# One more staging buffer, one more weight buffer and a new order for a chunked-attention and MoE kernel

## The chip, the cores and the metric

One Trainium2 chip, one of its cores. The metric is the device time of one execution in microseconds (us). Of the kernel before, three timed runs took 683.93, 684.89 and 685.61 us; the median is 684.89 us.

## The reference

Three stages follow each other, all in float32. The weights of the two feed-forward stages come to the kernel as 64-bit floats.

```
# 4 batches, 8 heads, 768 steps, 40 per head: gated recurrent attention
m_new = max(f + m, i); C = exp(f + m - m_new) * C + exp(i - m_new) * v k^T; n likewise with k
y = sigmoid(o_gate) * (C q) / max(|n q|, 1)
x = y as 3072 tokens x 320
x = ((x @ w1) * (x @ w2)) @ w3 @ w_out                          # d_ff 1024
out = max(max(x @ u1, x @ u2), x @ u3) @ u_out                  # d_ff 768
```

## The kernel before

**Units and visits.** The recurrence is done in chunks of 87 steps (`L`), nine per batch (the ninth has 72), so 36 units. `visit(v)` is one TensorE step: the scores of unit v (line 738) and the outputs and carried state of unit v - 1 (line 747). Both write one PSUM tile, `aq` (for the first odd units `acs`). DVE then multiplies the scores of unit v by its decays (line 772, into `pk`), which frees the tile for the scores of the next visit, and forms `y` from the outputs of unit v - 1 (lines 795 to 798; the gate is line 805, the copy of 64 columns lines 810 and 811). `pk` also needs the carried part, lines 696 and 705, on POOL or DVE. TensorE turns `y` (line 818), and ACT and DVE split the turned columns into a high and a low part (lines 836 and 839): these are the tokens of the feed-forward stages, in blocks of 384.

**Decays.** The gates of all 32 sequences are scanned on DVE at the start (lines 491 to 525). The result goes to DRAM (`d_na`, line 529), one batch of it comes back (line 561) and is split (lines 562 and 563), and the first nine units get their decays by matmuls (lines 656 and 657, the constant `one` from line 535) and an exponential on ACT (line 660). The other units load `d_na` (line 665) and use lines 670, 676 and 679.

**Weights.** A `granule` is 512 KB of 64-bit weights: one load (line 1050) into a staging buffer, two ACT steps or one ACT and one DVE step (lines 1055, 1061 or 1064), and a join on DVE (line 1072). Staging buffers are `sx` (three, only until the first switch of pools) and `stg` (three). `w3 @ w_out` is multiplied out on the chip: `fold(ft)`, eight times, each in two pieces of four float32 matmuls (line 1122); a piece needs one joined granule of `w3` in one of four buffers (`L_BUFS`), the first two pieces also the five granules of `w_out` in `wof`. Lines 1129 and 1133 empty each fold. The other weights are split into high and low parts (lines 1082 and 1085, 1097 and 1104).

**Feed-forward.** For each block of 384 tokens, groups of eight matmuls (lines 857 to 862) give the products with w1 and w2, or with u1 to u3; lines 903 and 905, or 931 and 934, combine them, lines 884 and 888 split the result, and lines 967 to 971 (first stage) or 986 (second) multiply on. `LATE`: weights of the second stage take the place of the pools `early` and `first` once nothing uses those (`late_w`).

**What sets the order.** Nothing is issued where the code stands. Every step is recorded by `Plan.op` with its engine, cost and dependencies, and `Plan.run` then walks a model of the engines and of the transfers (SP issues all of them from one queue; `LAND` is its time from the bus to the landing) and takes, on each free engine, the ready step of the lowest rank. `PRIO` holds a rank for each of 1963 steps, `PICK` a digit for each step that two engines can do. Each engine, SP too, executes its list in that order. The model's TensorE clock (`clock`) is slow up to a fixed time and full after it.

Of the kernel before, what the change touches and what calls it, by code (L numbers as in the profile page):

```python
# [43 lines left out]
EX = 3  # L44
L_BUFS = 4
# [11 lines left out]
LAND = 900  # L57
# [5 lines left out]
    "11011100110101111000011010001110000011001001110010100111001101101101011000000010111110111101001010111000110001"  # L63
    "00111001101101011010110001101100111100000110000111111101001111110011010111111100010100011110001100110011101101"
    "01011101001000101001110110101010100101111001110010000100011110001100101111001000010000010100000110100101111000"
    "10000000000111100000011100111110001001111010110101011000"
)
PRIO = (
# [100 lines left out]
def act(n, psum=False):  # L169
    return (51 if psum else 93) + 0.8333 * n  # L170
# [184 lines left out]
def mlstm_moe_kernel(  # L355
# [103 lines left out]
    for k_, n in (("msk", NCH * L), ("ff", NCH * L), ("aug", NCH * 128), ("git", NCH * L), ("gft", NCH * L)):  # L459
# [3 lines left out]
        for tag, (x, y) in where.items():  # L463
            if x < o + n and o < y:
                over[tag].append(("g", k_))
        o += n
    made["rv", 0], made["cr", 0] = misc[:, 0:8 * L], misc[0:L, o:o + 128 + LE]
    for tag, (x, y) in where.items():
        if x < 8 * L:
            over[tag].append(("rv", 0))  # L470
# [872 lines left out]
```

## Time and profile before

| | |
|---|---|
| three runs, median | 684.89 us (683.93 to 685.61) |
| profiled execution, its own time | 686.26 us |
| span of the profiled execution | 684.3 us |
| TensorE matmul (PE) busy | 655.6 us, 96% |
| weight load (PEld) busy | 621.1 us, 91% |
| DVE, ACT, POOL busy | 360.0, 296.8, 198.3 us |
| bytes moved | 76.09 MB, mean 111 GB/s |

Times inside the profile count from its first instruction; the profiled execution took 1.96 us more than its span, and 1.37 us more than the median. PE is the engine that matters, so the table is to be read by stretches of time and not by engine: where PE sits idle, and where its clock (PEclk, in tenths of 2.4 GHz) is below full. In the second table of the profile, the span in 40 slices of 17.1 us, PE is below nine tenths in the first, second, fifth and sixth slice and in the last, and PEclk in the fifth; the transfers keep their engines busy by seven tenths or more in the first five slices and by less after that.

### The profile page before, as it was taken

How to read it: one execution, taken by the hardware profiler on the slowest of the kernel's cores; microseconds unless marked ns; L12 is line 12 of the kernel's file. 1: busy time of each engine (PE TensorE's matmuls, PEld its weight loads, DVE VectorE, ACT ScalarE, POOL GpSimd, SP SyncE). 2: the span in 40 equal slices, each digit the busy share in tenths (PEclk: the TensorE clock that was granted, in tenths of full speed). 3: DMA queues.
4: the chain of work that ended last, by engine and by line, in shares of the span. 5: the costliest groups of instructions: out<-in, count | busy, mean ns of one | idle time of the engine just before them, and what ended most of it. 6: DMA issues, size and time to landing. Idle time of an engine off the chain costs nothing.

```text
span 684.3 us, 14869 instructions
## 1 busy us (share of the span) xinstructions
PE 655.6 (96%) x6217; PEld 621.1 (91%) x6217; DVE 360.0 (53%) x717; ACT 296.8 (43%) x572; POOL 198.3 (29%) x195
## 2 busy tenths in 40 slices
PE   3899889999999999999999999999999999999997
PEld 2577789999999999999999999999999999999997
DVE  7578797698745584453444464543345461312332
ACT  6856767677631345341423335344333232323202
POOL 1015444555421145122232353233232421010000
PEclk9999899999999999999999999999999999999999
DMA  8999735456322154221123172232032200000001
GB/s 304 330 330 368 252 115 182 148 185 187 110 83 95 55 159 148 84 83 41 44 83 113 46 210 88 64 104 76 8 112 84 86 8 1 2 1 0 1 1 58
DMA packets 25887, 76.09 MB, mean 111 GB/s; under 512 B 3260, under 2 KB 6899, under 8 KB 25820
## 3 DMA queue, kind: packets, MB, share of 16 engines
q1 hardware_dynamic: 25820, 75.14, 33.9%
q8 instruction: 48, 0.79, 0.5%
q14 instruction: 19, 0.16, 0.1%
HBM read 71.10 MB, written 4.03 MB: 110 GB/s over the span
## 4 chain that ended last, share of the span: by engine, by line
PE 83%; DMA 5%; DVE 5%; ACT 3%; issue 2%; POOL 1%; SPq 0%; ACTq 0%; POOLq 0%; DVEq 0%
PE wk L857 13%; PE wk L858 12%; PE wk L859 12%; PE acs L986 9%; PE wk L860 6%; PE wk L862 5%; PE acs L967 4%; PE acs L971 4%; PE wk L1122 4%; PE aq L747 3%; PE acs L969 3%; PE aq L738 3%; PE wk L872 1%; PE wk L818 1%; DMA sx<-in_wo 1%
## 5 line engine op out<-in xcount | busy, mean ns | idle before, releaser
L884 ACT CAST ph<-misc 128x384 fp32r<-128x384 f32 (+1 forms) x114 | 57.6, 508 | 169.2 <-PE acs L986 72.3
L888 POOL TENSOR_TENSOR pl<-misc,ph 128x384 fp32r<-128x384 f32 (+1 forms) x60 | 63.4, 1057 | 229.8 <-ACT ph L884 224.8
L934 DVE TENSOR_TENSOR misc<-misc,wk 128x384 f32<-128x384 f32 (+1 forms) x98 | 53.2, 545 | 104.5 <-PE wk L862 77.7
L857 PE MATMUL wk<-xh,wch 128*128 128x384 f32 x288 | 98.4, 342 | 1.7 <-DVE misc L934 1.0
L858 PE MATMUL wk<-xh,wcl 128*128 128x384 f32 x288 | 96.9, 336 | 0.0
L859 PE MATMUL wk<-xl,wch 128*128 128x384 f32 x288 | 96.8, 336 | 0.0
L857 PE MATMUL wk<-xh,wah 128*128 128x384 f32 x256 | 89.2, 349 | 2.6 <-DVE misc L905 1.1
L858 PE MATMUL wk<-xh,wal 128*128 128x384 f32 x256 | 87.0, 340 | 0.0
L859 PE MATMUL wk<-xl,wah 128*128 128x384 f32 x256 | 86.9, 339 | 0.0
L905 DVE TENSOR_TENSOR misc<-misc,wk 128x384 f32<-128x384 f32 x64 | 35.2, 551 | 81.6 <-PE wk L862 39.8
L857 PEld LDWEIGHTS wk<-xh,wch 128*128 128x128 f32 x288 | 54.1, 188 | 4.0 <-DVE misc L934 2.0
L903 ACT COPY misc<-wk 128x384 f32<-128x384 f32 x64 | 30.4, 476 | 61.5 <-PE wk L862 40.1
L888 DVE TENSOR_TENSOR pl<-misc,ph 128x384 fp32r<-128x384 f32 (+1 forms) x54 | 32.5, 604 | 44.6 <-ACT ph L884 44.4
L858 PEld LDWEIGHTS wk<-xh,wcl 128*128 128x128 f32 x288 | 54.1, 188 | 0.0
L859 PEld LDWEIGHTS wk<-xl,wch 128*128 128x128 f32 x288 | 54.1, 188 | 0.0
L857 PEld LDWEIGHTS wk<-xh,wah 128*128 128x128 f32 x256 | 48.8, 191 | 4.7 <-DVE misc L905 1.8
L1122 PE MATMUL wk<-wof,w 128*128 128x320 f32 x128 | 40.4, 472 | 12.6 <-DVE w L1072 11.7
L986 PE MATMUL acs<-wd,ph 128*128 128x320 f32 x288 | 51.0, 311 | 0.6 <-ACT misc L1028 0.5
L858 PEld LDWEIGHTS wk<-xh,wal 128*128 128x128 f32 x256 | 48.8, 191 | 0.0
L859 PEld LDWEIGHTS wk<-xl,wah 128*128 128x128 f32 x256 | 48.8, 191 | 0.0
L860 PE MATMUL wk<-xh,wcr 128*128 128x384 f32 x144 | 48.4, 336 | 0.0
L1122 PEld LDWEIGHTS wk<-wof,w 128*128 128x128 f32 x128 | 25.8, 206 | 23.5 <-DVE w L1072 11.8
(147 smaller groups left out, 1317.8 us busy)
## 6 DMA issues: line engine op xcount, KB each, us to landing
kv<-in_kv SPq DMA_DIRECT2D x32, 672.0 KB, 5.2
raw<-in_qk SPq DMA_DIRECT2D x36, 348.0 KB, 4.6
dd<-d_na SPq DMA_DIRECT2D x24, 348.0 KB, 4.0
sx<-in_w3t SPq DMA_DIRECT2D x9, 512.0 KB, 6.6
stg<-in_wc SPq DMA_DIRECT2D x9, 512.0 KB, 4.2
out<-misc SPq DMA_DIRECT2D x24, 160.0 KB, 2.2
stg<-in_w3t SPq DMA_DIRECT2D x7, 512.0 KB, 8.5
stg<-in_wa SPq DMA_DIRECT2D x5, 512.0 KB, 6.1
```

Of the source, the lines that this page charges most:

```text
L857: PE.matmul(p, lhsT=h_[:, kt], rhs=xh[:, kt], start=kt == 0, stop=False)
L858: PE.matmul(p, lhsT=l_[:, kt], rhs=xh[:, kt], start=False, stop=False)
L859: PE.matmul(p, lhsT=h_[:, kt], rhs=xl[:, kt], start=False, stop=False)
L860: PE.matmul(p, lhsT=r_, rhs=xh[:, 2], start=False, stop=False)
L862: PE.matmul(p, lhsT=r_, rhs=xl[:, 2], start=False, stop=True)
L884: P.op("A", act(n), lambda sl=sl: A.copy(out=T("ph", key)[:, sl], in_=T(*src)[:, sl]), r=[src + part], w=[("ph", key) + part])
L888: e.tensor_tensor(out=T("pl", key)[:, sl], in0=T(*src)[:, sl], in1=T("ph", key)[:, sl].bitcast(F32), op=ALU.subtract)
L903: P.op("A", act(TB, True), lambda: A.copy(out=T(*sa), in_=T(*ps[0])), r=[ps[0]], w=[sa])
L905: P.op("V", dve(TB), lambda: V.tensor_tensor(out=T(*sa), in0=T(*sa), in1=T(*ps[1]), op=ALU.mult), r=[ps[1]], w=[sa])
L934: P.op("V", dve(sl.stop - sl.start), lambda sl=sl: V.tensor_tensor(out=T(*sc)[:, sl], in0=T(*sc)[:, sl], in1=T(*ps)[:, sl], op=ALU.max), r ...
L986: PE.matmul(T(f"ac{m}", (k, 1)), lhsT=src[:, m * 128:m * 128 + 128], rhs=w[:, o:o + DM], start=first_, stop=last_,)
L1122: PE.matmul(T(*ps), lhsT=T(*w3)[:, i * 128:i * 128 + 128], rhs=wof[:, gt * 320:gt * 320 + 320], start=gt == 0, stop=gt == 7,)
```

## The change

`EX` goes from 3 to 4 and `L_BUFS` from 4 to 5: a fourth `sx` staging buffer and a fifth buffer for joined `w3`. The fourth `sx` lies in the pool `first`, so that the gate of the second set of late weights now also waits for the last use of `sx`. The load of the constants `sel` and its tile get 96 rows in place of 87. `LAND` goes from 900 to 1300, the modelled cost of the `kv` load from 1.3 to 1.36 per element, and `PICK` and `PRIO` are replaced in full. The columns recorded with a visit (`cols`) are not read by `run`.

```diff
-EX = 3
-L_BUFS = 4
+EX = 4
+L_BUFS = 5
...
-LAND = 900
+LAND = 1300
...
-    "11011100110101111000011010001110000011001001110010100111001101101101011000000010111110111101001010111000110001"
+    "10110100100101010111000001100000100101110111110011010011011011100000111101110010111101010110110010011011100100"
...
-    27, 139, 164, 433, 293, 56, 36, 192, 232, 29, 10, 114, 554, 467, 59, 73, 329, 383, 395, 148, 303, 652, 287, 664,
...
-        (early, "sx", EX, 1024), (tmp, "w3", L_BUFS, 512), (tmp, "raw0", RAW0, 8 * L),
+        (early, "sx", 3, 1024), (tmp, "sx", EX - 3, 1024), (tmp, "w3", L_BUFS, 512), (tmp, "raw0", RAW0, 8 * L),
...
-        slots[tag] = [pool_.tile([128, n], F32, name=f"{tag}{i}") for i in range(bufs)]
+        slots.setdefault(tag, []).extend(pool_.tile([128, n], F32, name=f"{tag}{pool_.id}_{i}") for i in range(bufs))
...
-    made["rv", 0], made["cr", 0] = misc[:, 0:8 * L], misc[0:L, o:o + 128 + LE]
+    made["rv", 0], made["cr", 0] = misc[:, 0:8 * L], misc[0:LP, o:o + 128 + LE]
...
-        dma(1.3 * m, lambda: SP.dma_start(out=T("kv", q)[:, 0:m], in_=kv[b, c, :, 0:m]), w=[("kv", q, x) for x in "kgx"])
+        dma(1.36 * m, lambda: SP.dma_start(out=T("kv", q)[:, 0:m], in_=kv[b, c, :, 0:m]), w=[("kv", q, x) for x in "kgx"])
...
-                if key[0] in (("raw", "sg", "w3", "wo", "mp") if q else ("hl", "one", "sx")):
+                if key[0] in (("raw", "sg", "sx", "w3", "wo", "mp") if q else ("hl", "one", "sx")):
...
-    sel = np.eye(L, 128 + LE, dtype=f)
-    sel[:, 128:] = np.where(np.arange(L)[:, None] > np.arange(LE), f(-1e30), f(0))
+    sel = np.eye(LP, 128 + LE, dtype=f)
+    sel[:, 128:] = np.where(np.arange(LP)[:, None] > np.arange(LE), f(-1e30), f(0))
```

The lists keep their lengths (PE 3171 rows, DVE 687, SP 183), and nearly every row moves. Of the steps that two engines can do, DVE now has 19 of line 696 (14 before), 56 of line 888 (52), 14 of line 705 (13), 17 of line 805 (20) and 7 of line 1029 (14). Three places follow; in the new kernel a tile's name also carries the number of its pool (`sx78_0` is the first `sx`, `w366_0` the first buffer of joined `w3`, `wk61_1` the second `wk`).

DVE at the start, from the join of the first `w_out` granule (`wof`) on; `w30` is the first joined `w3`, `mp` and lines 515 to 521 are the end of the gate scan. Before:

```order
L1072 SCALAR_TENSOR_TENSOR wof_75<-sx0_107 128x512
L506 SCALAR_TENSOR_TENSOR misc_122<-misc_122 32x783
L1072 SCALAR_TENSOR_TENSOR wof_75<-sx1_108 128x512
L1064 TENSOR_SCALAR sx2_109<-sx2_109 128x512
L1072 SCALAR_TENSOR_TENSOR w30_110<-stg2_106 128x512
L1072 SCALAR_TENSOR_TENSOR wof_75<-sx2_109 128x512
L515 SCALAR_TENSOR_TENSOR mp_76<-misc_122,mp_76 32x9
L525 COPY misc_122<-mp_76 32x9x41
L521 TENSOR_TENSOR misc_122<-misc_122,mp_76 32x783
```

and now:

```order
L1072 SCALAR_TENSOR_TENSOR wof_75<-sx78_0_107 128x512
L506 SCALAR_TENSOR_TENSOR misc_124<-misc_124 32x783
L515 SCALAR_TENSOR_TENSOR mp_76<-misc_124,mp_76 32x9
L521 TENSOR_TENSOR misc_124<-misc_124,mp_76 32x783
L1064 TENSOR_SCALAR sx78_1_108<-sx78_1_108 128x512
L525 COPY misc_124<-mp_76 32x9x41
L1072 SCALAR_TENSOR_TENSOR wof_75<-sx78_1_108 128x512
L1072 SCALAR_TENSOR_TENSOR w366_0_111<-stg58_1_105 128x512
L1072 SCALAR_TENSOR_TENSOR wof_75<-sx78_2_109 128x512
```

The end of the gate scan now stands ahead of the joins that TensorE's first fold piece needs.

PE just before its first feed-forward group, around the last three turns of `y` (line 818) that the first block of tokens needs. Before:

```order
L1122 MATMUL wk0_117<-wof_75,w32_112 128x320 x4
L1122 MATMUL wk0_117<-wof_75,w33_113 128x320 x4
L818 MATMUL wk1_118<-cs_73,misc_122 128x87 x3
L656 MATMUL wk2_119<-hl1_81,hl0_80 128x352
L657 MATMUL wk2_119<-one_82 128x352
L818 MATMUL wk1_118<-cs_73,misc_122 128x87 x3
L818 MATMUL wk2_119<-cs_73,misc_122 128x87 x3
L656 MATMUL wk0_117<-hl1_81,hl0_80 128x352
L657 MATMUL wk0_117<-one_82 128x352
L738 MATMUL aq0_120<-raw00_114 87x87 x8
```

and now:

```order
L1122 MATMUL wk61_0_119<-wof_75,w366_4_115 128x320 x4
L656 MATMUL wk61_2_121<-hl1_81,hl0_80 128x352
L657 MATMUL wk61_2_121<-one_82 128x352
L818 MATMUL wk61_1_120<-cs_73,misc_124 128x87 x3
L1122 MATMUL wk61_0_119<-wof_75,w366_0_111 128x320 x4
L818 MATMUL wk61_2_121<-cs_73,misc_124 128x87 x3
L818 MATMUL wk61_1_120<-cs_73,misc_124 128x87 x3
L738 MATMUL aq61_0_122<-raw066_0_116 87x87 x8
```

A fold piece of four matmuls now stands between the third and the fourth of the turns.

DVE after the outputs of visit 7, up to the product (line 772) that frees `aq` for visit 8. Before:

```order
L839 TENSOR_TENSOR xl1_88<-wk1_118,xh1_85 128x3x87
L795 TENSOR_SCALAR misc_122<-aq0_120 87x8
L796 SCALAR_TENSOR_TENSOR misc_122<-aq0_120,misc_122 87x8
L797 RECIPROCAL misc_122<-misc_122 87x8
L798 TENSOR_TENSOR misc_122<-aq0_120,misc_122 87x320
L905 TENSOR_TENSOR misc_122<-misc_122,wk0_117 128x384
L805 TENSOR_TENSOR misc_122<-misc_122,kv0_99 87x320
L1072 SCALAR_TENSOR_TENSOR stg0_104<-stg0_104 128x512
L783 COPY_PREDICATED kv1_100<-cs_73,aq0_120 63x8x41
L1104 TENSOR_TENSOR war_70<-sx2_109,war_70 64x4x128
L705 TENSOR_TENSOR pk1_98<-kv1_100,dd1_95 63x8x87
L772 TENSOR_TENSOR pk1_98<-aq0_120,dd1_95 87x8x87
```

and now:

```order
L783 COPY_PREDICATED kv58_1_100<-cs_73,aq61_0_122 63x8x41
L839 TENSOR_TENSOR xl58_1_88<-wk61_1_120,xh58_1_85 128x3x87
L905 TENSOR_TENSOR misc_124<-misc_124,wk61_0_119 128x384
L805 TENSOR_TENSOR misc_124<-misc_124,kv58_0_99 87x320
L1072 SCALAR_TENSOR_TENSOR stg58_2_106<-stg58_2_106 128x512
L1064 TENSOR_SCALAR stg58_1_105<-stg58_1_105 128x512
L1072 SCALAR_TENSOR_TENSOR stg58_1_105<-stg58_1_105 128x512
L705 TENSOR_TENSOR pk58_1_98<-kv58_1_100,dd58_1_95 63x8x87
L772 TENSOR_TENSOR pk58_1_98<-aq61_0_122,dd58_1_95 87x8x87
```

Lines 795 to 798 stand just ahead of the first of these rows. Two splits (line 1104 here, line 696 just before the first list) have left this stretch for POOL, and one more conversion (line 1064 and its join) has come into it.

## Rows read from the trace of the kernel before

**Rows 1.** The page's first table: busy us, share of the span, instructions.
```profile
PE 655.6 (96%) x6217; PEld 621.1 (91%) x6217; DVE 360.0 (53%) x717; ACT 296.8 (43%) x572; POOL 198.3 (29%) x195
```

**Rows 2.** Stretch, length; busy PE, PEld, DVE, ACT, POOL; PEclk, DMA share, GB/s.
```profile
0.00:11.32 11.32, 0.00 (x0) 0.00 (x1) 7.52 (x10) 6.16 (x9) 1.98 (x10) 1.00 0.79 288
11.32:29.70 18.38, 15.13 (x63) 9.86 (x63) 11.75 (x22) 16.90 (x28) 0.00 (x0) 1.00 1.00 324
29.70:76.91 47.21, 44.63 (x613) 33.09 (x613) 36.81 (x81) 30.52 (x60) 17.19 (x15) 0.94 0.95 344
76.91:100.00 23.09, 21.30 (x251) 20.32 (x247) 20.47 (x36) 14.46 (x28) 6.90 (x6) 0.84 0.44 141
100.00:684.30 584.30, 574.59 (x5297) 557.83 (x5295) 283.49 (x570) 228.75 (x449) 172.19 (x165) 1.00 0.26 81
```

**Rows 3.** PE in order of time, 0 to 62 us: start, length, [idle before <- releaser].
```profile
11.32 4.64 PE L1122 MATMUL wk<-wof,w 128*128 128x320 f32 x8 [11.32 <-DVE w L1072]
15.89 1.32 PE L570 MATMUL acs<-cs,misc 32*127 32x32 f32 x9
...
26.33 0.40 PE L656 MATMUL wk<-hl,hl 128*128 128x352 f32 x1 [1.21 <-ACT stg L1055]
...
28.25 0.40 PE L656 MATMUL wk<-hl,hl 128*128 128x352 f32 x1 [0.60 <-DVE wb L1133]
...
29.70 4.11 PE L1122 MATMUL wk<-wof,w 128*128 128x320 f32 x8 [0.89 <-ACT dd L660]
...
57.62 2.32 PE L1122 MATMUL wk<-wof,w 128*128 128x320 f32 x8
```

**Rows 4.** Busy time by stretch again, columns as in rows 2: inside three stretches.
```profile
29.90:33.20 3.30, 3.30 (x7) 2.13 (x7) 2.57 (x4) 2.26 (x6) 0.00 (x0) 0.50 0.96 350
...
74.30:81.00 6.70, 6.70 (x94) 6.45 (x94) 5.15 (x11) 4.48 (x11) 1.60 (x2) 0.50 0.55 167
...
94.80:98.10 3.30, 3.30 (x77) 3.07 (x74) 3.03 (x8) 0.51 (x1) 0.00 (x0) 0.50 0.77 181
```

**Rows 5.** PE in order of time, 60 to 110 us.
```profile
71.98 0.42 PE L818 MATMUL wk<-cs,misc 87*128 87x87 f32 x3 [0.67 <-DVE xl L839]
73.52 0.44 PE L818 MATMUL wk<-cs,misc 87*128 87x87 f32 x3 [1.12 <-ACT dd L660]
...
84.86 0.81 PE L747 MATMUL aq<-kv,pk 127*32 127x41 f32 x64
...
94.23 1.04 PE L738 MATMUL aq<-raw 40*87 40x72 f32 x16 [1.79 <-DVE pk L772]
```

**Rows 6.** DVE in order of time, 76 to 98 us.
```profile
85.90 1.61 DVE L696 TENSOR_TENSOR pk<-kv,dd 127x320 f32<-127x320 f32 x1
...
90.95 0.69 DVE L1104 TENSOR_TENSOR war<-sx,war 64x512 fp32r<-64x512 f32 x1
91.67 1.59 DVE L705 TENSOR_TENSOR pk<-kv,dd 63x696 f32<-63x696 f32 x1
93.30 0.88 DVE L772 TENSOR_TENSOR pk<-aq,dd 87x696 f32<-87x696 f32 x1
```

**Rows 7.** DVE in order of time, 0 to 62 us.
```profile
10.58 0.68 DVE L1072 SCALAR_TENSOR_TENSOR w<-stg 128x512 int32<-128x512 int32 x1
...
11.79 0.22 DVE L515 TENSOR_TENSOR_SCAN mp<-misc,mp 32x9 f32<-32x9 f32 x1
...
12.33 0.94 DVE L521 TENSOR_TENSOR misc<-misc,mp 32x783 f32<-32x783 f32 x1
```

**Rows 8.** Busy time by stretch once more, columns as in rows 2: 20 to 40 us.
```profile
20.00:40.00 20.00, 17.15 (x72) 11.56 (x71) 11.00 (x22) 15.87 (x28) 0.00 (x0) 0.91 1.00 357
```

**Rows 9.** Transfers, 0 to 60 us, in 40 slices of 1.5 us.
```profile
GB/s 0 92 307 350 393 382 426 407 415 320 280 246 254 214 390 325 332 299 404 382 317 378 384 368 367 410 366 214 277 341 377 352 183 363 279 372 405 416 426 414
```

**Rows 10.** Groups by line and shape, the whole span: busy us, mean ns.
```profile
L696 DVE TENSOR_TENSOR pk<-kv,dd 127x320 f32<-127x320 f32 x12 | 9.4, 781 | 0.0
...
L1064 DVE TENSOR_SCALAR sx<-sx 128x512 int32<-128x512 int32 x7 | 3.0, 425 | 1.7 <-DMA sx<-in_w3t 1.5 <-DMA sx<-in_wo 0.2
```

More of the change, by code (lines that the diff above doesn't have):

```diff
@@ L62 @@
 PICK = (
-    "11011100110101111000011010001110000011001001110010100111001101101101011000000010111110111101001010111000110001"
-    "00111001101101011010110001101100111100000110000111111101001111110011010111111100010100011110001100110011101101"
-    "01011101001000101001110110101010100101111001110010000100011110001100101111001000010000010100000110100101111000"
-    "10000000000111100000011100111110001001111010110101011000"
+    "10110100100101010111000001100000100101110111110011010011011011100000111101110010111101010110110010011011100100"
+    "11001010111110011110111010001110001001001110111100010011101010011011010101001000010010000000101101101100100110"
+    "10000010011111110010010100111100001110000101011001101011000010100000100010111000111001100111100101000100000011"
+    "01011010010011011110000111101100011011110011011100010000"
 )
 PRIO = (
[95 rows of a table removed]
[95 rows of a table added]
 )
@@ L533, in mlstm_moe_kernel @@
     P.op("G", 400, lambda: G.memset(T("hl", 1)[64:128].bitcast(F32), 0.0), w=[("hl", 1, 2), ("hl", 1, 3)])
-    P.op("A", act(128 + LE), lambda: A.copy(out=T("one", 0), in_=T("cr", 0)), r=[("cr", 0)], w=[("one", 0)])
+    P.op("A", act(128 + LE), lambda: A.copy(out=T("one", 0), in_=T("cr", 0)[0:L]), r=[("cr", 0)], w=[("one", 0)])
     P.op("A", act(NCH * 128), lambda: A.copy(
@@ L768, in visit @@
             r += [("y", turned), ("cs", 0)]
-        P.op("P", ns, f, cols=200 + 110 * bool(turned), r=r, w=w, early=early)
+        P.op("P", ns, f, cols=200 + 110 * bool(turned) + TB * bool(pair), r=r, w=w, early=early)
         if v < NU:
```

189 rows, old and new, of the table PRIO are left out of this document.

## The prediction

> **What bounds the kernel now.** I read the page first: PE is busy for 655.6 of 684.3 us [rows 1], so at most some 29 us can be won, and the question is where they lie. The table by stretch answers that [rows 2]. From 100 us on PE is busy for 574.59 of 584.30 us at full clock, and DVE for less than half of that time: nothing there can give much. Before 11.32 us PE has no work; from there to 100 us it is idle for 7.6 us, and its clock is at the lower level, 1.2 GHz, in three stretches [rows 4]. In each of these PE is busy without a break at a granted clock of 0.50, so half of the stretch is lost: 1.65, 3.35 and 1.65 us. What PE did before the clock fell is in order of time: idle for 0.60 and 0.89 us just before the first [rows 3], 0.67 and 1.12 us before the second, 1.79 us before the third [rows 5]. So a wait of some 1.5 to 1.8 us costs itself and about as much or twice as much again in clock. The waits name what ended them: the emptying of a fold, the decays' exponentials, the split of turned tokens, and DVE's line 772, which frees the tile that the next visit writes. The profiled execution took 686.26 us, 1.37 more than the median of the runs; the sum below is made against 686.26.
>
> **The buffers.** The two buffers add no instruction and no byte. They let SP issue one load earlier and DVE join one granule earlier. Their use lies in the first 60 us, where the transfers run at 324 to 344 GB/s with their engines busy at 0.95 to 1.00 [rows 2]; there are gaps that a further buffer could fill, down to 214 GB/s near 20 us [rows 9]. I cost the buffers alone at nothing: after 30 us PE is 44.63 of 47.21 us busy, so it takes its data later than they land. The 96 rows of `sel` and its earlier load cost nothing either: ACT reaches its copy behind other loads that must land first.
>
> **The order, start.** PE's first piece starts when the first joined `w3` is there, at 11.32 us. DVE's list now puts the end of the gate scan (lines 515, 521, 525) ahead of that join; these took from 11.79 to 13.27, 1.48 us [rows 7]. So PE starts by 1.1 to 1.5 us later, near 12.5. Against that, line 521 ends near 10.6 in place of 13.27, so the round trip of the decays through DRAM starts 2.7 us earlier, and the decay matmuls, which PE waits for at 26.33 (1.21 us), can come sooner. Line 570 (1.32 us [rows 3]) is put off, so PE still owes it when the third fold begins. I take the third fold (29.70 us now) to begin about 1 us sooner with 1 us more to do: **0**. Bounds: +1.5 (the late start paid in full) and -2.7 (the gates' lead gained in full).
>
> **First half-clock stretch.** The new list still has decay matmuls that wait for ACT's table load and exponentials just before the third fold, so I let the waits and the 1.65 us stand: **0** (bound -1.65). The same holds for the later decay matmuls: again they follow a fold piece whose tile they take over.
>
> **The last turns before the first group.** Now three turns follow almost at once, each waits for the split of the one before: 0.67 and 1.12 us [rows 5]. In the new list a fold piece lies between the third and the fourth; such a piece took 2.32 us at full clock [rows 3], more than either wait. The fifth turn still waits for the split of the third, which stands in DVE's list behind two rows of line 1104, a line 705 and a line 772. I leave 0.8 of the 1.79 us: **-1.0** (bounds 0 and -1.79). With so little idle the clock need not fall: **-3.35** (bound 0) [rows 4].
>
> **Visit 8.** The outputs of visit 7 end at 85.67 us, PE is ready for visit 8 at 92.44 and gets the tile at 94.23 [rows 5]. DVE spent that time on one list of rows. Of it line 696 (1.61 us) and line 1104 (0.69) are now POOL's, and a conversion and its join come in, 0.43 and 0.68 us [rows 6, 7, 10]. From 85.67 to the end of line 772 at 94.18 are 8.5 us; less 2.3, plus 1.1, that is 7.3. PE needs 6.8 for what lies between. A wait of 0 to 0.6 is left; I take 0.6: **-1.2** (bounds 0 and -1.79). Then the third fall of the clock goes too: **-1.65** (bound 0).
>
> **What the new order adds.** The four terms make -7.2 us. But the whole list was drawn anew, and its model knows no fall of the clock after the first rise, so it has no reason to avoid two short waits side by side. The old order, drawn in the same way, has 7.6 us of idle and 6.65 of half clock between 11.32 and 100 us. I followed the new rows at the places above and can't exclude such waits at others. Bounds: nothing, or all of the 7.2 given back; nothing in the rows decides between them, so I take the middle, **+3.6**. After 100 us I take no change (bounds -2 and +2: 9.7 us of idle are there now, and the last visits and evacuations stand as before).
>
> **Sum.** 0 + 0 - 1.0 - 3.35 - 1.2 - 1.65 + 3.6 = -3.6; 686.26 - 3.6 = 682.7 for a profiled execution, **681.3** for the median.
>
> **Rivals.**
> 1. *The transfers set the pace and the gain is lost.* Visit 1 stands earlier in PE's list, before the second half of fold 2. Its q and k block is now the 23rd transfer, 9.5 MB into SP's list (by the sizes in that list). By rows 2, 9.2 MB are moved by 29.70 us and the 9.5 by 30.6; PE comes to it near 33. At the 288 GB/s of the first stretch it would be 33.0, and with the landing PE would wait for up to 2 us, with 1.65 of clock behind it: +3.6, so 685, no change. For it: 1.00 busy at 357 GB/s from 20 to 40 us [rows 8]. Against: single slices of up to 426 GB/s [rows 9], so 357 is no ceiling here. The Trainium skill ("DMA: Bandwidth & Descriptors", Specifications) gives about 358 GB/s as HBM's limit per core, by which no buffer could bring a byte earlier between 20 and 40 us and this rival would be the likeliest, at 685; the slices speak against it as a hard limit. Chance 0.18.
> 2. *Slower: DVE late at visits 6 to 9.* By the new lists DVE has 5 more of line 696 (0.78 us [rows 10]) and 4 more of line 888; against them stand 7 fewer evacuations, near the end of each block. Between 76.91 and 100 us it is busy for 20.47 of 23.09 already [rows 2]. If line 772 ends 1.8 us after PE is ready at three of these visits, each costs 1.79 and 1.65: 10.3 us, in place of the 8.6 that the two places cost now (1.79 + 3.35 + 1.79 + 1.65); with the late start paid, +1.5, that is +3.2, **688**. It decides between a wait of 1.2 us, which passed at 26.33 without a fall at once, and the 1.79 at 94.23, which didn't. Against it: the visit that I could count through comes out earlier. Chance 0.14.
> 3. *All of it.* No new waits: -7.2 or a little more from later stages, 677. For it: every place I counted through improves. Chance 0.14.
>
> **Chances and range.** The forecast has 0.54. A measurement here can tell about 0.3%, 2.05 us, from no change: faster is below 682.8, slower above 686.9. The forecast lies 1.5 us below the first bound; I give four fifths of it and all of rival 3 to faster, with a little of rival 1: 0.62. The rest of the forecast and nearly all of rival 1: 0.23 the same. Rival 2 and the tail of rival 1: 0.15 slower. The range goes from rival 3 to just past rival 1 and the nearer half of rival 2: 676.5 to 687.
>
> **What would show it.** Right: the first piece near 12.5 us; the third fold near 28.7; the first group (line 857, 76.91 now) at 72 to 75; no granted clock of 0.50 between 60 and 100 us, idle before visit 8 under 0.7; the time past 100 us within 2 us of 584.3. Wrong: PE waiting for `raw` or `kv` loads before 60 us (rival 1), two or more waits on line 772 over 1.5 us each with the clock at 0.50 behind them (rival 2), or a difference that arises after 100 us, for which I have no term.

## The result and the profile after

The changed kernel takes **675.26 us** (674.08 to 676.97, 4 executions) against 684.41 us for the kernel before beside it (680.74 to 685.61, 4 executions): a ratio of 0.9877, 95% interval 0.9834 to 0.9921. That is 9.2 us faster where 3.6 were forecast, and 1.2 us below the forecast range. Later, beside the experiments, both were run again: before at 682.9, 682.9 and 683.3 us (29, 23 and 17 executions), the changed kernel at 676.1 and 674.2 (4 each). One of the 23 took 800.97 us at a mean granted clock of 0.754 and is left out of all that follows. Over all 12 of its executions the changed kernel has a median of 675.3, so the better figure for the change is **-7.6 us**. The three runs that the forecast was made against (684.89) lay 2.0 us above the later 682.9; counted from 682.9, the forecast range would begin at 674.5 and hold the result. The size is missed either way: 3.6 forecast, 7.6 to 9.2 measured. The profiled execution after took 675.12 us, its span is 673.4.

The first table of the page after, which answers to [rows 1]:

```profile
PE 652.2 (97%) x6217; PEld 618.1 (92%) x6217; DVE 358.1 (53%) x715; ACT 297.8 (44%) x576; POOL 190.3 (28%) x193
```

The stretches that answer to [rows 2], cut at the same events: the first piece, the third fold, the first group, 100 us (columns as in rows 2).

```profile
0.00:12.57 12.57, 0.00 (x0) 0.00 (x0) 8.78 (x12) 6.04 (x9) 1.93 (x10) 1.00 0.82 273
12.57:29.87 17.30, 14.75 (x54) 8.99 (x54) 10.47 (x19) 15.99 (x27) 0.00 (x0) 0.94 1.04 348
29.87:74.67 44.80, 44.80 (x625) 34.05 (x625) 35.94 (x76) 30.29 (x62) 18.78 (x15) 0.95 0.92 335
74.67:100.00 25.33, 24.84 (x340) 23.22 (x340) 22.72 (x42) 19.14 (x38) 9.84 (x11) 1.00 0.71 243
100.00:673.40 573.40, 567.84 (x5202) 551.87 (x5200) 280.17 (x567) 226.37 (x444) 159.73 (x159) 1.00 0.25 79
```

From the third fold to the first group PE is now busy without a break, 44.80 of 44.80 us. PE in order of time, as in [rows 3, 5]:

```profile
26.73 0.43 PE L656 MATMUL wk<-hl,hl 128*128 128x352 f32 x1 [1.66 <-DVE hl L563]
...
29.87 4.63 PE L1122 MATMUL wk<-wof,w 128*128 128x320 f32 x8
...
71.84 0.61 PE L818 MATMUL wk<-cs,misc 87*128 87x87 f32 x6
...
74.67 0.34 PE L857 MATMUL wk<-xh,wah 128*128 128x384 f32 x1
...
88.94 0.84 PE L738 MATMUL aq<-raw 40*87 40x72 f32 x16 [0.29 <-DVE pk L772]
```

Both turn waits of [rows 5] are gone (71.84, no wait) and visit 8 waits 0.29 us in place of 1.79. At the start one wait is longer, 1.66 us at 26.73 where it was 1.21 at 26.33, but those at 28.25 and 29.70 are gone in this execution: between its first piece and the third fold PE is idle for 2.55 us (17.30 less 14.75) in place of 3.25. Two windows of the changed kernel, as in [rows 4]:

```profile
27.82:34.65 6.83, 6.74 (x28) 4.52 (x25) 3.23 (x7) 4.32 (x8) 0.73 (x1) 0.50 1.02 380
60.00:100.00 40.00, 39.51 (x559) 35.02 (x558) 35.14 (x70) 32.55 (x65) 17.55 (x15) 1.00 0.80 277
```

Behind that wait the clock is at half for 6.83 us, twice as long as in the kernel before; from 60 to 100 us it does not fall at all.

What the prediction had no term for is the time past 100 us. What PE waited for there, us in total, times, longest; first the kernel before, then the changed one:

```profile
PE wk L857 <- DVE misc L905: 1.1, 2, 0.7
PE wk L857 <- DVE misc L934: 1.0, 2, 0.7
PE acs L967 <- ACT xh L1008: 1.0, 1, 1.0
PE wk L857 <- ACT misc L903: 0.7, 2, 0.5
PE wk L857 <- DVE xl L839: 0.7, 1, 0.7
PE wk L857 <- ACT misc L931: 0.5, 2, 0.3
PE acs L986 <- ACT misc L1028: 0.5, 1, 0.5
```

```profile
PE acs L967 <- DVE misc L1020: 0.5, 2, 0.3
PE acs L986 <- ACT misc L1028: 0.5, 1, 0.5
PE wk L857 <- ACT misc L931: 0.3, 1, 0.3
```

Eleven waits of 5.5 us in all have become four of 1.3. None was above 1.0 us, so none stands out in the page; together they are more than the 3.58 us of waits that the prediction costed at the turns and at visit 8.

### The profile page after: what moved, and what is told of

The parts are those of the page before. It is cut to its first block, busy times and chain, and to the rows that moved or that the text cites. A ratio compares the mean times of both kernels' runs of the same rounds, so it can differ in the third digit from the quotient of the medians.

```text
span 673.4 us, 14869 instructions
## 1 busy us (share of the span) xinstructions
PE 652.2 (97%) x6217; PEld 618.1 (92%) x6217; DVE 358.1 (53%) x715; ACT 297.8 (44%) x576; POOL 190.3 (28%) x193
## 5 line engine op out<-in xcount | busy, mean ns | idle before, releaser
L888 POOL TENSOR_TENSOR pl<-misc,ph 128x384 fp32r<-128x384 f32 (+1 forms) x57 | 59.7, 1049 | 202.3 <-ACT ph L884 196.4
L903 ACT COPY misc<-wk 128x384 f32<-128x384 f32 x64 | 30.5, 478 | 70.4 <-PE wk L862 43.7
L888 DVE TENSOR_TENSOR pl<-misc,ph 128x384 fp32r<-128x384 f32 (+1 forms) x57 | 34.4, 603 | 48.7 <-ACT ph L884 48.1
L931 ACT COPY misc<-wk 128x384 f32<-128x384 f32 x48 | 23.1, 480 | 64.5 <-PE wk L862 52.4
```

The lines of the kernel that those rows point to most:

```text
L888: e.tensor_tensor(out=T("pl", key)[:, sl], in0=T(*src)[:, sl], in1=T("ph", key)[:, sl].bitcast(F32), op=ALU.subtract)
L903: P.op("A", act(TB, True), lambda: A.copy(out=T(*sa), in_=T(*ps[0])), r=[ps[0]], w=[sa])
L931: P.op("A", act(TB, True), lambda: A.copy(out=T(*sc), in_=T(*ps)), r=[ps], w=[sc])
```

## The experiments

All but f0 and e5, which are the changed kernel itself, take the order from a written list of steps (`SEQ`) and engines (`ENG`). The buffers are those of the changed kernel. The other edits of the change, as the 96 rows of `sel`, are in all of them. So the order can be set piece by piece, and a "seam" is the step at which one kernel's list goes over to the other's:

```diff
-        for t, j, fn in order:
+        for t, j, fn in [(0, j, ops[j][2][ops[j][0].index(e)]) for j, e in zip(SEQ, ENG)]:
             fn()
```

The opposite of e1, the new list with the old buffers, was not run. So the experiments show what the buffers bring to the old list, and not what the new list would be worth without them. The edits of e1 to e4 and of e6 are given in words.

**e1: the buffers alone.**

```diff
-EX = 3; L_BUFS = 4; order by the ranks of before
+EX = 4; L_BUFS = 5; SEQ = the same order, step by step
```

> The list of the kernel before, instruction by instruction, with the fourth staging and the fifth weight buffer. Order theory (the gain comes from the new list alone): 684.4 us, within 0.3% of before; the same three stretches at half clock below 100 us. Buffer theory (loads and joins held back by a buffer set the pace): loads go out earlier, PE's third fold begins over 1 us before 29.70 and the time is 682 or less.

Measured: 681.89 us (677.94 to 684.89, 12 executions), ratio 0.9981 [0.9956, 1.0005]. The buffers bring nothing to the old list that the measurement can tell, at most 3 us of the 7.6. (681.89 also meets the "682 or less" of the buffer theory, but its other sign is not there: the third fold begins at 31.63, later than the 29.70 of before.) Its trace shows something else (windows, columns as in rows 2; then PE in order of time):

```profile
18.21:25.03 6.82, 6.82 (x18) 4.83 (x18) 2.27 (x5) 6.15 (x10) 0.00 (x0) 0.50 0.85 257
72.83:79.64 6.81, 6.81 (x95) 6.17 (x95) 5.16 (x12) 4.35 (x11) 2.26 (x3) 0.50 0.67 253
94.80:98.10 3.30, 3.30 (x39) 3.25 (x27) 3.15 (x9) 0.99 (x2) 0.27 (x1) 1.00 0.89 235
```

```profile
17.86 1.78 PE L570 MATMUL acs<-cs,misc 32*127 32x32 f32 x9 [2.29 <-DMA cs<-in_cst]
...
93.41 0.84 PE L738 MATMUL aq<-raw 40*87 40x72 f32 x16 [1.80 <-DVE pk L772]
...
112.05 0.45 PE L857 MATMUL wk<-xh,wah 128*128 128x384 f32 x1 [0.98 <-ACT misc L903]
```

The list is that of before and the wait of visit 8 is the same 1.80 us, but no fall of the clock follows it, nor one at 30 us, while there is one at 18 us that the kernel before did not have. That one comes just behind a wait of 2.29 us for the constants `cst`, which before does not have either; in the traces of e2, e4, e7 and e8, which also start with the old list on the new buffers, PE waits 0.46 to 1.16 us there. So the buffers are not without effect at the start. Visit 8 is the cleaner case: of the four traces in which PE waits 1.8 us there (before, e1, e4, e7) the clock falls behind it in two (before and e4). At the turns, of the five traces with the waits of the old list (before, e1, e4, e7, e8), it falls in four, for 6.83, 6.83, 3.41 and 3.41 us. The falls are not fixed to the list, but they are far from evenly spread.

**e2, e3, e4, e6: half of each list.**

```diff
-SEQ = one kernel's order
+e2: SEQ = before up to PE's 36th step (some 60 us), then what is left in the new order
+e3: SEQ = new up to a visit near 104 us (112 in before), then what is left in the order of before
+e4: SEQ = before up to that visit, then what is left in the new order
+e6: SEQ = new up to a step near 191 us (200 in before), then what is left in the order of before
```

> The list of before up to PE's 36th group (the last half fold but one, about 60 us in, where both kernels have done the same PE work), and from there the list of the changed kernel. Theory of separate places: in the traces the new list has lost about 1 us by then, so this gives back that 1 us: 674.3. Rival (the later gain of the new list rests on what its own first 60 us have staged): waits appear behind the seam and the time is 676 or more.

Measured: 677.32 us (676.24 to 680.16, 6 executions), 0.9932 [0.9910, 0.9953]: the rival is right. Behind the seam a wait appears that neither kernel has in this form:

```profile
71.15 0.64 PE L818 MATMUL wk<-cs,misc 87*128 87x87 f32 x6 [1.85 <-ACT dd L660]
```

So by this trace the new list wins at the turns only together with its own start: the two places do not add.

> The list of the changed kernel up to a visit that begins near 104 us in it (112 before), where both have done the same PE work, then the list of before. By the two traces 6.9 us are won up to there. Theory that the other 4 us also come from the list: 684.4 - 6.9 = 677.5. Theory that those 4 us are scatter between two executions or come from buffers: 674 to 675.5, as the changed kernel.

Measured: 682.28 us (680.55 to 684.80, 12 executions), 0.9997 [0.9981, 1.0013], as slow as before, a value that neither theory gave. By its trace it is 6.2 us ahead of before at the seam and 7.0 soon after, when before has waited 0.54 us, and then loses 5.3 of these:

```profile
124.15 0.79 PE L971 MATMUL acs<-pl,wb 128*128 128x384 f32 x3 [1.53 <-POOL pl L888]
128.75 0.69 PE L857 MATMUL wk<-xh,wah 128*128 128x384 f32 x1 [1.71 <-ACT misc L903]
```

```profile
126.10:132.90 6.80, 5.09 (x75) 4.93 (x62) 4.11 (x7) 5.50 (x13) 3.74 (x3) 0.50 0.57 175
```

A PE that is earlier meets the order of ACT and POOL of before, in which its inputs come no sooner; the gain is given back in waits and, in this execution, in the half clock of the window above. The run says nothing on what the first 100 us are worth.

> The reverse: the list of before up to that visit, then the new list. If the new list also saves waits after 100 us: 684.4 - 4 = 680.4. If not (scatter, or my term of nothing after 100 us): 684.4, within 0.3%. If the gains of the two halves add, the savings of this and of the kernel with the new list up to 100 us sum to the 9.2 us between the two kernels.

Measured: 680.15 us (677.37 to 683.14, 12 executions), 0.9964 [0.9945, 0.9983], 2.8 us below the 682.9 of before (1.2 to 3.8). The 4 us that the two traces gave are just above that interval, and nothing at all is below it: the new list also wins past 100 us. Against e1, which has the same buffers, the median is only 1.7 us lower, and the two scatter over 677 to 685 us, so it is the traces that carry this. (e3's 0.6 us and e4's 2.8 do not add up to the 7.6 of the whole.) Its waits there (view as above) are those of the changed kernel and one of 0.4:

```profile
PE acs L986 <- ACT misc L1028: 0.5, 1, 0.5
PE acs L967 <- DVE misc L1020: 0.5, 2, 0.3
PE acs L986 <- ACT ph L884: 0.4, 1, 0.4
PE wk L857 <- ACT misc L931: 0.2, 1, 0.2
```

> The new list up to a piece of work near 191 us in it (200 before), then the list of before; a quieter seam than at 104 us, where the list of before ran into waits of 1.5 and 1.7 us behind the seam. In the traces 8.9 of the 10.9 us are won by then: if the places add, 682.9 - 0.82 x 7.6 = 676.7 by the medians. If every seam costs as the one at 104 us did: 680 or more.

Measured: 675.28 us (673.97 to 680.77, 6 executions), 0.9902 [0.9870, 0.9934]. At this quieter seam nothing is lost, and up to 200 us the new list has already won all that the medians can tell. The waits of before past 200 us are back in its trace; they cost it some 1.5 us against the changed kernel's trace, which the scatter of so few executions hides.

**e5 and f0: the changed kernel again.**

> The changed kernel once more, for more executions beside the same runs of before. Theory that the falls of the clock are the list's doing: half clock in the same place (27.8 to 34.7) and the same length in nearly every execution, time 675.3. Theory that a short wait only gives a chance of a fall: the time at half clock, worked out from the mean granted clock of each execution, differs by whole stretches of 3.4 us between executions, and the time scatters with half of that.

> The changed kernel again, as the base of the three kernels beside it: 675.3 to 676.1 us, some 6 us of it at half clock.

Measured: 676.13 us (675.23 to 676.43) and 674.23 us (672.27 to 675.71), 4 executions each; f0 is just below the base that was written for it, and its half clock, 3.0 us on the mean, is half of the 6 that was written. The trace of e5 has the same 6.83 us at half clock near 28 us; f0 has the same wait (1.57 us for line 563) and no half clock while PE works:

```profile
16.20:668.00 651.80, 644.83 (x6213) 614.04 (x6211) 346.38 (x699) 288.75 (x561) 189.05 (x183) 1.00 0.33 109
```

The mean granted clock of each execution gives its time at half clock (span x 2 x (1 - clock); the end of the span, 0 to 2.8 us in the traces, is included, though it lies behind the last matmul and costs nothing): in the 12 executions of the changed kernel from 0 to 8.1 us, mean 4.8; in 68 executions of before from 4 to 19 us, mean 8.6. The second theory is right: one and the same list has its falls in some executions and not in others, and sets only how likely they are.

**e7: a fold piece between the turns.** PE's list alone:

```diff
 L1122 MATMUL wk_0_119<-wof,w_4_115 128x320 x4
+L818 MATMUL wk_1_120<-cs,misc 128x87 x3
 L1122 MATMUL wk_0_119<-wof,w_0_111 128x320 x4
-L818 MATMUL wk_1_120<-cs,misc 128x87 x3
 L656 MATMUL wk_2_121<-hl_81,hl_80 128x352
```

> The list of before (buffers as in the changed kernel) with one edit on PE: half a fold piece (line 1122, 8 matmuls) goes from ahead of a turn (line 818) to behind it. Prediction's term taken at its word: 0.67 to 1.0 of the two waits of 0.67 and 1.12 us goes, and the fall of the clock behind them with its 3.35: 681.9 - 4 = 677.5. Theory of chance falls: the wait goes, the time falls by 0.7 to 1.5 on the mean, and half clock shows up in other places.

Measured: 682.10 us (679.08 to 685.42, 12 executions), 0.9995 [0.9974, 1.0016]. Both theories were wrong, since the waits stay:

```profile
70.76 0.41 PE L818 MATMUL wk<-cs,misc 87*128 87x87 f32 x3 [0.47 <-DVE xl L839]
72.26 0.44 PE L818 MATMUL wk<-cs,misc 87*128 87x87 f32 x3 [1.09 <-ACT dd L660]
```

0.47 and 1.09 us in place of 0.67 and 1.12: by the engines that end the waits, DVE and ACT come to the split and to the exponential when their own lists let them, and an earlier turn alone hardly changes that. A piece on PE was no cover here, where the lists of the engines that are waited for stayed.

**e8: two rows from DVE to POOL ahead of visit 8.** In DVE's list (they reappear in POOL's):

```diff
-L696 TENSOR_TENSOR pk_1_98<-kv_1_100,dd_1_95 127x8x40
...
-L1104 TENSOR_TENSOR war<-stg_1_105,war 64x4x128
 L705 TENSOR_TENSOR pk_1_98<-kv_1_100,dd_1_95 63x8x87
 L772 TENSOR_TENSOR pk_1_98<-aq_0_122,dd_1_95 87x8x87
```

> The list of before (same buffers) with two instructions given from DVE to POOL, as the new list has them: line 696 of visit 8 and one of line 1104, 2.3 us of DVE ahead of the line 772 that PE waits for at visit 8. Prediction's term: the wait of 1.8 us falls to under 0.6 and its fall of the clock goes, 681.9 - 1.2 - 1.65 = 679. Theory of chance falls: -1.2 to -2, so 680 to 680.7. Rival: POOL gives the row of line 696 later than DVE did, the wait stays: 681.9.

Measured: 681.38 us (679.55 to 682.10, 12 executions), 0.9969 [0.9950, 0.9989], which is 0.5 below e1, between the 680 to 680.7 of the theory of chance falls and the 681.9 of the rival. The wait is gone, as the prediction counted; of the time little is:

```profile
89.40 0.84 PE L738 MATMUL aq<-raw 40*87 40x72 f32 x16
...
107.74 0.44 PE L857 MATMUL wk<-xh,wah 128*128 128x384 f32 x1 [1.19 <-ACT misc L903]
```

Reckoned as in the table below, its trace is 1.8 us ahead on the work of visit 8 and 1.1 behind on the 80 us after it. The wait of 1.19 us shown stands in e1 too, with 0.98 (at 112.05), so only 0.2 of the loss is there. By the medians, too, most of the gain is given back; but the scatter of 12 executions (e1 alone: 677.94 to 684.89) leaves room for all of the 1.8, so this is likely and not shown.

**f1: the gates first on ACT.**

```diff
+L562 CAST hl_81<-misc 9x8x87
 L582 ACT_TABLE_LOAD
-L582 ACTIVATE sg_83<-sg_83 96x320 x3
+L582 ACTIVATE sg_83<-sg_83 96x320 x2
 L1129 CAST wb<-wk_0_119 128x320
-L562 CAST hl_81<-misc 9x8x87
-L582 ACTIVATE sg_83<-sg_83 96x320
+L582 ACTIVATE sg_83<-sg_83 96x320 x2
```

> The changed kernel with four instructions moved in the first 27 us: on ACT line 562 goes ahead of the table load and three sigmoids of line 582 (one of these goes behind the evacuation of line 1129), on DVE line 563 goes ahead of line 1133. Theory (the 2.6 us by which the gates' scan comes sooner are lost on ACT, where line 562 stands behind the sigmoids, and PE waits 1.4 to 1.7 us for line 563): the wait goes and the time falls by 1 to 1.5, with a fall of the clock fewer by up to 3: 672 to 674.5. Rival (the line's data isn't there sooner, or the start is bounded by the loads): the wait moves to the next decay matmul or fold piece, 675.5.

Measured: 676.08 us (675.98 to 677.29, 4 executions), 0.9910 [0.9878, 0.9942]: my theory falls, the rival is right. PE no longer waits for line 563, but up to the third fold there are now three other waits, 2.85 us in all, where f0 beside it has 1.57, 0.45 and 0.44:

```profile
25.71 0.40 PE L656 MATMUL wk<-hl,hl 128*128 128x352 f32 x1 [1.12 <-ACT sg L582]
27.95 0.40 PE L656 MATMUL wk<-hl,hl 128*128 128x352 f32 x1 [0.89 <-DVE wb L1133]
29.35 4.63 PE L1122 MATMUL wk<-wof,w 128*128 128x320 f32 x8 [0.84 <-ACT dd L660]
```

**f2 and f3: the price of a wait.** In the changed kernel, at nine (f2) and ten (f3) places past 200 us, one group of PE goes ahead of one (f2), or mostly two (f3), others; no other engine's list is touched. One of the nine:

```diff
-L967 MATMUL acs<-ph_1_91,wb 128x384 x3
-L969 MATMUL acs<-ph_1_91,wb 128x384 x2
-L971 MATMUL acs<-pl_1_93,wb 128x384 x3
 L857 MATMUL wk_1_120<-xh_0_84,wah 128x384
...
 L860 MATMUL wk_1_120<-xh_0_84,war 128x384
+L967 MATMUL acs<-ph_1_91,wb 128x384 x3
+L969 MATMUL acs<-ph_1_91,wb 128x384 x2
+L971 MATMUL acs<-pl_1_93,wb 128x384 x3
```

> The changed kernel with nine of PE's groups between 210 and 570 us moved ahead of one other group, 33 us or more apart, so that PE comes to each 0.7 to 0.9 us before its input: 6.7 us of waits in all by the trace of the changed kernel. Same work, same lists on the other engines. If short single waits cost only themselves: 675.6 + 6.7 = 682.3, half clock as in the changed kernel. If each can also bring the clock down for 3.4 us: up to 9 x 1.7 more, 697.

> The same with ten longer waits, 1.5 to 2.2 us each, 18.6 us in all. If waits cost only themselves: 675.6 + 18.6 = 694. By the price in the prediction (each wait of 1.5 to 1.8 us brings a fall that costs 1.65 to 3.35 more): 711 to 728. If a fall comes by chance, in one wait out of two: near 703, and executions differ by whole stretches of 3.4 us at half clock.

What PE waited for from 205 to 580 us in f2 (the two waits on line 1020 are in the changed kernel too):

```profile
PE wk L857 <- DVE misc L934: 2.7, 4, 0.7
PE wk L857 <- ACT misc L903: 2.3, 4, 0.6
PE wk L857 <- ACT misc L931: 0.9, 1, 0.9
PE wk L857 <- DVE misc L905: 0.7, 1, 0.7
PE acs L967 <- DVE misc L1020: 0.5, 2, 0.3
```

f2 measured 681.91 us (680.69 to 684.27, 12 executions): 6.6 us above the 675.3 of the changed kernel (7.7 above f0 beside it), for ten new waits of 6.6 us. Mean time at half clock 3.1 us (f0: 3.0), and none in six of twelve. **Single waits of 0.6 to 0.9 us, amid dense matmuls, brought no further half clock.** That the two 6.6 agree is in part luck: the changed kernel's twelve had 1.7 us more half clock (worth 0.8), and in the trace of f2 the PE work of 160 to 620 us (as in the table below) takes 8.7 us longer than in the changed kernel's. The idle time shown is less than a wait costs: matmuls of such a group start 0.18 us apart and are shown 0.34 long (their ends are modelled), so 0.16 us of each wait are hidden, and from the start of the matmul behind a wait to the next one it is 0.28. That makes some 0.27 us more for each wait, an estimate from the traces of f2 and f3.

From 200 to 640 us in f3, and its two stretches at half clock there (another begins behind the last matmul):

```profile
PE wk L857 <- DVE xl L839: 6.6, 4, 2.0
PE wk L857 <- DVE misc L905: 4.0, 3, 2.1
PE wk L857 <- DVE misc L934: 3.6, 2, 1.8
PE acs L967 <- ACT misc L1028: 1.8, 1, 1.8
PE wk L857 <- ACT misc L931: 1.2, 2, 0.6
PE wk L857 <- ACT xh L836: 0.7, 1, 0.7
PE wk L857 <- ACT misc L903: 0.6, 1, 0.6
PE acs L967 <- DVE misc L1020: 0.5, 2, 0.3
```

```profile
313.72:317.13 3.41, 3.41 (x13) 3.41 (x12) 0.00 (x0) 0.00 (x0) 0.00 (x0) 0.50 0.18 50
569.72:573.13 3.41, 3.41 (x11) 3.41 (x12) 0.00 (x0) 0.00 (x0) 0.51 (x1) 0.50 0.00 0
```

f3 measured 699.31 us (699.16 to 699.88, 4 executions): 24.0 us above the changed kernel (25.1 above f0), for 14 new waits of 18.5 us. Its mean time at half clock is 11.2 us, 6.4 more than the changed kernel's 4.8, worth 3.2 us; 14 times the 0.27 of above makes 3.8, and the three together 25.5, near what was measured. So nine waits of 1.2 to 2.1 us bring two falls in the traced execution, and such a wait, single and amid dense matmuls, costs on the mean some 0.35 us of clock (3.2 over nine), not 1.65 to 3.35. All three sums that were written down for f3 are missed: the nearest is 703, which took one fall in two waits where there was one in five. This price does not hold at the turns, where two waits (0.67 and 1.12 us) follow each other within 2 us: in the five traces of the old list there (under e1) the falls take 4.1 us on the mean, worth 2.0. Why the turns are so much more likely to bring one, no run here separates.

## Why the prediction was right, and where it was wrong

To compare executions I give each matmul its median time, which makes 625 us of PE work in each kernel, and read from the traces when the same amount is done. Half of every half-clock stretch is taken off and stands in rows of its own. Of the old list: the kernel before, e1 and e7, and e4, e8, e2 up to where they differ; of the new: its three traces, and e3 and e6 up to their seams.

| PE work, us | old list, us (range) | new list, us (range) | difference | forecast |
|---|---|---|---|---|
| until PE starts | 11.9 (11.3 to 12.3) | 12.8 (12.6 to 13.2) | +1.0 | start, with the next row: 0 |
| 0 to 36 | 42.9 (41.5 to 45.2) | 41.9 (41.1 to 42.6) | -0.9 | |
| 36 to 50 (turns) | 16.5 (16.5 to 16.5) | 14.3 (14.3 to 14.3) | -2.2 | -1.0 |
| 50 to 60 | 10.3 (10.0 to 10.9) | 10.9 (10.5 to 11.7) | +0.6 | new waits: +3.6 |
| 60 to 78 (visit 8) | 21.8 (21.0 to 22.4) | 20.3 (20.1 to 20.6) | -1.5 | -1.2 |
| 78 to 160 | 87.1 (86.9 to 87.3) | 84.8 (84.1 to 85.2) | -2.3 | 0 |
| 160 to 620 | 477.2 (476.9 to 477.5) | 475.5 (475.4 to 475.6) | -1.7 | 0 |
| half clock up to 36 | 1.7 (0 to 3.4) | 2.4 (0 to 3.4) | +0.7 | 0 |
| half clock from 36 | 3.0 (1.7 to 5.1) | 0 (all) | -3.0 | -3.35 - 1.65 = -5.0 |

The sum is -9.3; over all executions it is -7.6, of which 1.9 is clock by the means above. The traces are few, some of the old list among them had more half clock than most, and the rows other than clock, -7.0 here, are nearer -5.7 by the executions. The last row of work is the least sure: counting in what carries either list behind its seam (e3, e6, e8; e2, e4), the old list and the new overlap there, and the difference is nearer -1.1.

- **The step that failed is "After 100 us I take no change".** PE's idle time there (9.7 us in [rows 2], of which 5.5 are waits and 3.8 lie behind the last matmul) was read, and dismissed because the last visits stand as before. The table gives -4.0 past 78 us of work (-3.4 with the caution above), e4 alone -2.8 in the median. Taking 0 there, with bounds of 2 us, is the largest error of the sum. Each of the eleven waits is short, and each waits for a row of DVE or ACT, whose lists were drawn anew; that was in the trace and was not asked for. The sign that the prediction named for this, a time past 100 us within 2 us of 584.30, was ill made, since whatever is won before 100 us also shortens it (the forecast itself would have given 580.7); the 573.40 measured holds both, and the split by PE work is what shows the step wrong.
- **"What the new order adds": +3.6 was too much.** What is new or longer is 1.66 us at 26.73, paid for by shorter waits beside it, and one wait of 0.86 on line 903 near 76 us in one of the three traces (f0); the rows above give +0.6, and +0.7 of clock. The middle between the bounds was a guess and said so.
- **The falls of the clock, -5.0, were sized from one execution.** [rows 4] show three falls; e1, with the same list and the same waits at the turns and at visit 8, has one of these at the turns, none at 30 us and none at visit 8. The profiled execution was one with much half clock. In the traces the fall at the turns is worth 2.0 on the mean where 3.35 was taken, that of visit 8 0.85 (two of four) where 1.65 was. Over all executions the time at half clock goes from 8.6 to 4.8 us, worth 1.9. The direction was right, the term was too large; with the +3.6 it left -1.4, near the -1.9 by accident.
- **Start: 0 was right**, and so was its make-up: PE starts at 12.57 (12.5 foretold) and makes the 1 us good. The third fold came at 29.87 where 28.7 was foretold, but 1.0 us of that is the half clock from 27.82 on; in f0, which has none, it came at 28.93. And f1 shows that the gates' lead isn't to be had by moving their two rows alone.
- **Turns: -1.0 was too little** (-2.2, both waits gone), and the reason given is not enough: e7 shows that the fold piece between the turns alone isn't the cover. That DVE's and ACT's lists are is what the waits' ends suggest; their rows were not moved alone. The two waits were 1.79 us as shown, and with 0.27 for each 2.3.
- **Visit 8: right**, 0.29 us of wait where 0 to 0.6 was foretold, and e8 shows that the two rows given to POOL do it. What the prediction did not ask is whether the rest of a list keeps such a gain; in e8, on the old list, little of it is left by the medians.
- **Rival 1 (transfers) was wrong.** PE waits for no `raw` or `kv` load before 60 us. The changed kernel moves 380 GB/s over the 6.83 us of its window above. So the 358 GB/s that the Trainium skill lists as a core's limit ("DMA: Bandwidth & Descriptors", Specifications) is no ceiling for this one core; here the measurement decides. **Rival 2** was wrong: no wait on line 772 above 0.29. **Rival 3**, all of it at 677, was the nearest, and even it had only "a little" for the later stages.

Not shown: why 78 to 160 is won step by step. The waits that are gone are known and stay away in all three of its traces; the single moves of DVE and ACT that removed each were not tried one by one.

## What to carry to other kernels

Add up the short waits of a long steady stretch before calling it full: eleven waits of up to 1 us were worth about as much here (-3.4 to -4.0 us past 78 us of work) as the turns and visit 8 with the clock left out (-3.7). Before costing a fall of the clock, read the mean clock of several executions; one profile shows one draw. And in a list that was drawn as a whole, don't expect a gain at one place to stay: e3 gave 5.3 of 7.0 us back at waits on ACT and POOL, whose lists were the old ones, and in half clock, f1 exchanged one wait for three, and e8 kept little of its 1.8 by the medians.

## What was not expected of the hardware

The same list runs for 4 us at half clock in one execution and for up to 19 in another (68 executions of before), worth 2 to 9 us, and traces of one list show stretches of 3.41 or 6.83 us at a place where others show none. The Trainium skill ("TensorE: Matmul & The Clock Gate", Part 1, on the clock gate) says, of the slow matmuls at a kernel's start, that the chip's watch over TensorE runs free of that start, so that the same kernel meets it differently from run to run. The traces agree, and show it in the middle of a kernel: the changed kernel has 6.83 us near 28 us in two traces and none in f0, behind waits of 1.36 to 1.66 us. New is the price: single waits of 0.6 to 0.9 us amid dense matmuls, no further half clock in f2; of 1.2 to 2.1 us, two falls for nine waits in f3's trace; two waits of 0.67 and 1.12 us close together at the turns, a fall in four of five traces.
